# A planned one-core kernel (delta-rule attention and two feed-forward layers): counting instruction blocks in every group

## The chip, the cores and the metric

The program runs on one core of a Trainium2 chip. The metric is the device time of one execution in microseconds (us). Before the change it is 1174.78 us, the median of 3 runs (1173.24 to 1175.62).

## The reference

```python
# attention: B, H, S, D = 4, 8, 768, 48; a state matrix of 48x48 for each of 32 heads, step by step in time
k_n = k / (norm(k) + 1e-06)
for t in range(S):
    y[:, :, t] = einsum('bhd,bhde->bhe', q[:, :, t], state)
    v_old = einsum('bhde,bhd->bhe', state, k_n[:, :, t])
    state = state + beta[:, :, t] * einsum('bhd,bhe->bhde', k_n[:, :, t], v[:, :, t] - v_old)
x = y as 3072 tokens of 384
# first feed-forward layer, 1536 wide
x = (silu(x @ w_gate) * (x @ w_val)) @ moe_w_out
# second, 2048 wide
h = x @ w_in
out = where(h > 0, h, exp(min(h, 0)) - 1) @ moe2_w_out
```

The weights come as 64-bit floats and are taken apart on the chip.

## The kernel before

**Tiling.** The 3072 tokens are worked on in 12 groups g of 256. A group is 128 time steps of two batches, which makes 16 heads (u), cut into four chunks (c) of 32 steps that lie on the four 32-row quarters of the 128 partitions. `a` is the batch within the group, `par` the parity of a head.

**Attention steps of a group**, each one call of `add`: loads of k, q, v; norms of k (`norm`, L453 to L500); transposes of q and k on PE (tr, L538); products of k with k and q (gram, L570), masked by DVE into `gr`; inversion of the 32x32 triangles on DVE (`invert`, L630/L637, in groups 0 to 2 the half-size form L647/L653, joined by products j1 at L678 and j2 at L694); x (L741); g (`gstep`, L761), whose result is copied to `lc` (L770, a helper `put`); the chain of states over the chunks (L795, DVE adds at L801); y (L829); transposes of y (xtr, L853), which give the feed-forward input `xh`, `xl`. These are float32 products on 32-row corners of the array: each stands in the trace as two loads of weights and two products.

**Feed-forward.** `moe1` gives 24 projections (L995, runs of 9 products 128x256) and 12 output products (L1021, runs of 9) for each group. `moe2` (L1107, L1144) runs behind all groups.

**What sets the order.** Nothing is issued as it is written. `add` records a step with the engines that may do it and its readers and writers, and `Order.run` plans all engines' orders with its own times. `wait` orders a step behind the readers of a name as well, `r` only behind its last writer. PE's instruction stream is counted in blocks of 256 (`BLOCK`, counter `at`, a load and a product being two). `fetch(t, occ, n, keep)` says how late a step would come if it passes into a block that has not arrived; before the change it returns 0 for every time after `UNTIL` = 170e3 ns. Where a PE step would come over `STALL` late, `run` takes a short feed-forward step instead, if there is one. `JOIN` names kinds of steps (2: transposes, 4: chain, 5: y) whose two halves (a = 0, 1) are one step in groups after the first. Before 170 us the planner fills idle time of PE with products that nobody reads: `fill` (L1174, 128x512) and `fill2` (L1184), and ahead of a gap of over 6 us `quick` (L1179, 61 products of 16 columns), which runs the stream up to the next block's limit.

Of the kernel before, what the change touches and what calls it, by code (L numbers as in the profile page):

```python
# [45 lines left out]
class Order:  # L46
# [54 lines left out]
    def fetch(self, t, occ, n, keep):  # L101

        at, full, late = self.at, self.full, 0.0
        if t > self.until:
            return 0.0
        if not keep:
            full = dict(full)
        x = t
        end = at + n
        while at // self.BLOCK != end // self.BLOCK:  # L110
            b = at // self.BLOCK + 1
            x += occ * (b * self.BLOCK - at) / n
            at = b * self.BLOCK
            w = max(0.0, full.get(b, 0.0) - x)
            late += w
            x += w
            m = at - self.LEAD
            if m >= self.at:
                y = t + occ * (m - self.at) / n
            else:  # L120
                y = next((a + (m - k) * d for k, a, d in reversed(self.past) if k <= m), x)
            y = max(y, full.get(b, 0.0))
            full[b + 1] = y + self.FETCH[y < self.wire]
        if keep:
            self.past = self.past[-40:] + [(self.at, t, occ / n)]
            self.at = end
        return late

    def run(self, until):
# [22 lines left out]
        while left:  # L152
            best = {}
            for o in ready:
                for e, occ, lat, k, f in o.alts:
                    t = start_of(o, e, occ, lat, k)
# [27 lines left out]
            if e == "PE" and self.fill and t < self.until and left > 1:  # L184
                gap = t - free.get("PE", 0.0)
                if gap > 6000 and k[1] >= 128:
                    n = (self.BLOCK - self.at % self.BLOCK) // 2 + 1
                    self.fetch(t - gap, 28.0 * n, 2 * n, True)
                    self.quick(n)
                    gap -= 28.0 * n  # L190
                n = int(self.share * gap / self.unit)
                if n > 0:
                    late = self.fetch(t - gap, gap, 2 * n, True)
                    t = max(t, t - gap + n * self.unit + late)
                    self.fill(n)
                    kind[0] = k[0]
# [37 lines left out]
def delta_moe_kernel(ctx: ExitStack, tc: tile.TileContext, q, k, v, beta,  # L234
# [11 lines left out]
    C = 4  # L246
# [1 line left out]
    PL1 = 2.5  # L248
    ND = 10
    UNTIL = 170e3  # L250
    JOIN = (2, 4, 5)
    AHEAD = 3
    PAUSE = (0, 'x')
    HOLD = (0, 'm')
# [70 lines left out]
    def act(n, f, psum=True):  # L325
        return [("ACT", (75 if psum else 110) + .8333 * n, (165 if psum else 190) + .8333 * n, 0, f)]
# [4 lines left out]
    def pe(ns, f, kind=0, n=18):  # L331
        return [("PE", ns, ns + 160, (kind, n), f)]
# [115 lines left out]
    def prepare(g, p):  # L448
# [5 lines left out]
        def norm(u0, u1, keys):  # L454
# [12 lines left out]
            add(p, dve(n, lambda: V.tensor_reduce(out=ss[:, u], in_=sq[:, u], op=ALU.add, axis=AX.X)),  # L467
                r=part + ALLA[:3], w=[("ss", x) for x in keys])

            if two:  # L470
                add(p, act(u1 - u0, lambda: A.activation(out=r[:, u], in_=ss[:, u], func=ACTF.Sqrt), False),
                    r=[("ss", x) for x in keys] + ["sqrt"], w=[("sm", x) for x in keys])

# [243 lines left out]
    def attention(g, p):  # L717
# [32 lines left out]
        for a in range(2):  # L750
            for par in range(2):
                h = [Slots(AT if g else AT0, 1) for c in range(C)]

                def gstep(a=a, par=par, h=h):
                    if par == 0:
                        new_lc(a)()
                    for s in range(4):
                        u = a * 8 + 2 * s + par
                        for c in range(C):
                            t = slice(32 * c, 32 * c + 32)  # L760
                            PE.matmul(bank[h[c].got[0]][0:96, s * 80:s * 80 + 80], lhsT=R[t, u, :],  # L761
                                      rhs=gr[t, u, 0:80], start=True, stop=True, skip_group_check=True)
                add(p, pe(860, gstep, 3, 64), r=[(x, n) for x in ("Rk", "Rv") for n in (2 * a, 2 * a + 1)] + [("grk", a), ("grq", a, par)],
                    w=h + ([] if par else lk[a]), need=h,
                    wait=[("lc", a, par, c) for c in range(C)] + (lk[a] if par else []))
                for c in range(C):
                    def put(e, a=a, par=par, c=c, h=h[c]):
                        def f():
# [1 line left out]
                            e(out=buf['lc', a][par][:, :, c, :], in_=pv)  # L770
                        return f

                    add(p, act(320, put(A.copy)) + ([] if g else dve(320, put(V.tensor_copy))), r=[h[c]] + lk[a], w=[("lc", a, par, c)], use=[h[c]])

                def plus(a=a, par=par):
                    b = 64 * par
# [398 lines left out]
                      start=True, stop=True, skip_group_check=True)  # L1175

    def quick(n):
        for _ in range(n):
            PE.matmul(acc[:, 0, 0:16], lhsT=identr, rhs=identr[:, 0:16], start=True, stop=True,  # L1179
                      skip_group_check=True)  # L1180

    def fill2(n):
# [87 lines left out]
```

## Time and profile before

| | |
|---|---|
| median of 3 runs | 1174.78 us (1173.24 to 1175.62) |
| profiled execution, own time | 1170.46 us |
| its span, first to last instruction | 1168.8 us |
| PE busy | 1133.6 us, 97% |
| DVE busy | 779.1 us, 67% |
| ACT busy | 569.3 us, 49% |
| first groups (0 to 170 us), PE busy | 153.84 of 170 us |
| groups with moe1 (170 to 765 us), PE busy | 581.87 of 595 us |
| moe2 (765 to 1168.8 us), PE busy | 397.89 of 403.8 us |

PE is busy nearly all the time, but a busy PE is not at its peak: its small products last some 200 ns each and overlap, so a stretch is read by when the next product starts. Idle time marked "issue" is time in which PE waited for no semaphore that the profile shows. PEclk is the granted clock as a share of 2.4 GHz; it has the levels 0.5 and 1.0.

### The profile page before, as it was taken

To read this page: it belongs to the slowest core of one execution; us is meant where nothing else is said; L and a number is where in the kernel's file an instruction comes from. 1 tells how busy PE (TensorE), PEld (TensorE's weight loads), DVE (VectorE), ACT (ScalarE), POOL (GpSimd) and SP (SyncE) were. 2 spreads that over 40 slices of the span, in tenths; PEclk is the share of its full clock that TensorE was granted. 3 is DMA by queue.
4 is the path that set the end of the run, shared out by engine and by line. 5 is a ranking of instruction groups with operands and counts; after the bars stand their busy time and mean duration, and the time that the engine had idled before them with its cause. 6 is when DMAs were issued, how large, how long until landed. Compare 5 with 4: busy or idle time off the path is not lost.

```text
span 1168.8 us, 34176 instructions
## 1 busy us (share of the span) xinstructions
PE 1133.6 (97%) x14707; PEld 1048.5 (90%) x14707; DVE 779.1 (67%) x2429; ACT 569.3 (49%) x1119; POOL 47.9 (4%) x62
## 2 busy tenths in 40 slices
PE   8889999999999999999999999999999999999998
PEld 7688989998999898989998999989888889888887
DVE  6799858696868686768787743996545344454444
ACT  6599442524242424343434343996545454454443
POOL 2200000000010000000000000000000000000000
PEclk8999999999999999999999999999999999999999
DMA  9480202112020202020200003900101001010000
GB/s 207 127 269 16 43 12 44 33 30 43 16 43 15 44 15 43 9 50 15 44 15 17 15 3 116 371 19 28 55 1 55 1 19 36 1 36 1 27 1 28
DMA packets 106855, 57.34 MB, mean 49 GB/s; under 512 B 76976, under 2 KB 101552, under 8 KB 106704
## 3 DMA queue, kind: packets, MB, share of 16 engines
q1 hardware_dynamic: 106704, 55.16, 17.7%
q8 instruction: 115, 1.88, 0.7%
q14 instruction: 36, 0.29, 0.1%
HBM read 45.71 MB, written 9.44 MB: 47 GB/s over the span
## 4 chain that ended last, share of the span: by engine, by line
PE 86%; DVE 6%; ACT 4%; issue 2%; DMA 1%; SPq 0%; ACTq 0%; DVEq 0%
PE gv L995 24%; PE acc L1021 11%; PE acc L1144 8%; PE at L1144 8%; PE gv L1107 8%; PE at L1107 8%; PE at L761 3%; PE at L795 3%; PE at L741 3%; PE at L570 2%; PE at L829 2%; PE at L538 2%; PE acc L1174 1%; PE acc L1179 1%; DVE ain L661 1%
## 5 line engine op out<-in xcount | busy, mean ns | idle before, releaser
L995 PE MATMUL gv<-xh,w 128*128 128x256 f32 x1728 | 292.6, 288 | 2.0 <-ACT tb L1002 1.4
L995 PEld LDWEIGHTS gv<-xh,w 128*128 128x128 f32 x1728 | 240.0, 191 | 9.0 <-ACT tb L1002 2.0
L1021 PE MATMUL acc<-hb,w 128*128 128x256 f32 x1296 | 184.8, 288 | 0.7 <-issue 0.7
L1021 PEld LDWEIGHTS acc<-hb,w 128*128 128x128 f32 x1296 | 167.8, 194 | 6.2 <-issue 3.7
L995 PE MATMUL gv<-xl,w 128*128 128x256 f32 x864 | 150.6, 283 | 0.3 <-DVE xl L862 0.3
L1002 ACT ACTIVATE tb<-gv 128x256 f32<-128x256 f32 x144 | 55.5, 385 | 189.9 <-PE gv L995 189.9
L995 PEld LDWEIGHTS gv<-xl,w 128*128 128x128 f32 x864 | 124.0, 191 | 0.5 <-DVE xl L862 0.5
L1005 DVE TENSOR_TENSOR tb<-gv,tb 128x256 f32<-128x256 f32 x144 | 60.5, 420 | 78.9 <-ACT tb L1002 51.1
L1009 ACT CAST hb<-tb 128x256 fp32r<-128x256 f32 x144 | 58.7, 407 | 111.5 <-DVE tb L1005 111.5
L1122 DVE SCALAR_TENSOR_TENSOR hb<-gv,hb 128x512 f32<-128x512 f32 x48 | 33.2, 691 | 91.5 <-ACT hb L1119 91.5
L637 DVE TENSOR_TENSOR z<-z,ain 128x60 f32<-128x60 f32 (+32 forms) x522 | 88.5, 209 | 1.1
L630 DVE TENSOR_TENSOR ain<-z,ain 128x60 f32<-128x60 f32 (+32 forms) x522 | 87.7, 205 | 1.0
L1122 DVE SCALAR_TENSOR_TENSOR hb<-at,hb 128x512 f32<-128x512 f32 x48 | 33.1, 690 | 81.0 <-ACT hb L1119 80.9
L1012 DVE TENSOR_TENSOR hb<-tb,hb 128x256 fp32r<-128x256 f32 x144 | 63.9, 444 | 18.4 <-ACT hb L1009 17.7
L1113 ACT ACTIVATE hb<-gv 128x512 f32<-128x512 f32 x48 | 28.7, 597 | 96.5 <-PE gv L1107 96.4
L1119 ACT ACTIVATE hb<-hb,neg 128x512 f32<-128x512 f32 x96 | 69.5, 724 | 2.7
L1113 ACT ACTIVATE hb<-at 128x512 f32<-128x512 f32 x48 | 28.7, 597 | 79.4 <-PE at L1107 79.1
L1116 ACT ACTIVATE hb<-hb 128x512 f32<-128x512 f32 x96 | 60.8, 633 | 2.8
L761 PE MATMUL at<-gr,R 32*96 32x80 f32 x1488 | 45.8, 251 | 0.0
L761 PEld LDWEIGHTS at<-gr,R 32*96 32x96 f32 x1488 | 38.1, 159 | 7.0 <-ACT w L770 0.4
L1144 PE MATMUL acc<-w,ain 128*128 128x384 f32 x192 | 39.6, 340 | 1.8 <-DVE ain L1127 1.3
L1107 PE MATMUL gv<-lc,w 128*128 128x512 f32 x144 | 41.0, 394 | 0.0
(205 smaller groups left out, 2110.6 us busy)
## 6 DMA issues: line engine op xcount, KB each, us to landing
w<-in_moe_w_out_dram SPq DMA_DIRECT2D x28, 384.0 KB, 6.8
w<-in_moe_w_in_dram SPq DMA_DIRECT2D x16, 384.0 KB, 5.8
R<-in_v_dram SPq DMA_DIRECT2D x24, 192.0 KB, 2.8
w<-in_moe_w_gate_dram SPq DMA_DIRECT2D x12, 384.0 KB, 7.5
w<-in_moe_w_val_dram SPq DMA_DIRECT2D x12, 384.0 KB, 7.9
qp<-in_q_dram SPq DMA_DIRECT2D x11, 384.0 KB, 4.7
kp<-in_k_dram SPq DMA_DIRECT2D x11, 384.0 KB, 4.8
x2d<-hb SPq DMA_DIRECT2D x12, 256.0 KB, 2.0
```

The source lines that it names most:

```text
L630: V.tensor_tensor(out=t, in0=z[:, l:l + 1, x:y].to_broadcast([128, l, y - x]), in1=an[:, l, 0:l].unsqueeze(2).to_broadcast([128, l, y - x] ...
L637: V.tensor_tensor(out=z[:, 0:l, x:y], in0=z[:, 0:l, x:y], in1=t, op=ALU.add)
L761: PE.matmul(bank[h[c].got[0]][0:96, s * 80:s * 80 + 80], lhsT=R[t, u, :], rhs=gr[t, u, 0:80], start=True, stop=True, skip_group_check=True)
L995: PE.matmul(dst, lhsT=wt[:, a_, kk * 128:(kk + 1) * 128], rhs=xx[:, kk, :], start=(n == 0), stop=(n == 3 * KD - 1))
L1005: V.tensor_tensor(out=c['s'], in0=bank[h.got[0]][:, TB:2 * TB], in1=c['s'], op=ALU.mult)
L1012: return lambda: e.tensor_tensor(out=c['h'][:, 1, :], in0=c['s'], in1=c['h'][:, 0, :].bitcast(F32), op=ALU.subtract)
L1021: PE.matmul(o_, lhsT=w[:, a_, d * 128:(d + 1) * 128], rhs=c['h'][:, b_, :], start=(f == 0 and n == 0 and d != 1), stop=(f == F1 - 1 and n ...
L1107: PE.matmul(x, lhsT=W[f][:, 0, a_, kk * 128:(kk + 1) * 128], rhs=x2[n][b_][:, kk, :], start=(m == 0), stop=(m == 3 * KD - 1))
L1116: A.activation(out=c['r'], in_=c['r'], func=ACTF.Exp, scale=-1.0)
L1119: A.activation(out=c['r'], in_=c['r'], func=ACTF.Identity, bias=neg1, scale=1.0)
L1122: V.scalar_tensor_tensor(out=c['r'], in0=bank[h.got[0]], scalar=0.0, in1=c['r'], op0=ALU.max, op1=ALU.add)
L1144: PE.matmul(o, lhsT=c['h'][:, b_, t * 128:(t + 1) * 128], rhs=W[f][:, 1][:, a_, :], start=(f == 0 and m == 0), stop=(f == F2 - 1 and m == 2))
```

## The change

It has five parts. `fetch` counts blocks at all times, and when it only asks (keep False) it adds how late the following block would come, were the rest of the block run at 59 ns an instruction. `quick` issues float32 products of 32x32 corners with 16 columns in place of 128x128 ones, half as many calls, and its count is rounded. `JOIN` keeps the chain alone, so that transposes and y are planned in halves. `norm` of group 1 takes a square root on ACT as group 0 does, where it had Newton steps on DVE. `gstep` with par = 1 waits for the last writer of `lc` and not for its readers, and the copies of g's result may go to DVE as well as to ACT in every group.

```diff
@@ fetch
-        if t > self.until:
-            return 0.0
...
             y = max(y, full.get(b, 0.0))
             full[b + 1] = y + self.FETCH[y < self.wire]
+        if not keep:
+            b = at // self.BLOCK + 1 if at == end else end // self.BLOCK + 1
+            rest = (b * self.BLOCK - end) * 59.0
+            return late + max(0.0, full.get(b, 0.0) - (t + occ + late) - rest)
@@ run
-                    n = (self.BLOCK - self.at % self.BLOCK) // 2 + 1
+                    n = (self.BLOCK - self.at % self.BLOCK) // 4 * 2 + 2
                     self.fetch(t - gap, 28.0 * n, 2 * n, True)
                     self.quick(n)
@@
-    JOIN = (2, 4, 5)
+    JOIN = (4,)
@@ norm
-            if two:
+            if g < 2:
                 add(p, act(u1 - u0, lambda: A.activation(out=r[:, u], in_=ss[:, u], func=ACTF.Sqrt), False),
@@ gstep
-                add(p, pe(860, gstep, 3, 64), r=[(x, n) for x in ("Rk", "Rv") for n in (2 * a, 2 * a + 1)] + [("grk", a), ("grq", a, par)],
+                add(p, pe(860, gstep, 3, 64), r=[(x, n) for x in ("Rk", "Rv") for n in (2 * a, 2 * a + 1)] + [("grk", a), ("grq", a, par)] + (lk[a] if par else []),
                     w=h + ([] if par else lk[a]), need=h,
-                    wait=[("lc", a, par, c) for c in range(C)] + (lk[a] if par else []))
+                    wait=[("lc", a, par, c) for c in range(C)])
...
-                    add(p, act(320, put(A.copy)) + ([] if g else dve(320, put(V.tensor_copy))), r=[h[c]] + lk[a], w=[("lc", a, par, c)], use=[h[c]])
+                    add(p, act(320, put(A.copy)) + dve(320, put(V.tensor_copy)), r=[h[c]] + lk[a], w=[("lc", a, par, c)], use=[h[c]])
@@ quick
-        for _ in range(n):
-            PE.matmul(acc[:, 0, 0:16], lhsT=identr, rhs=identr[:, 0:16], start=True, stop=True,
+        for x in range(n // 2):
+            r = slice(32 * (x % 4), 32 * (x % 4) + 32)
+            PE.matmul(acc[r, 0, 0:16], lhsT=ident[r, r], rhs=ident[r, 0:16], start=True, stop=True,
```

In the changed file every line from 104 to 121 stands two lower, and from 122 on two higher in number (L761 is L763), at the end three (L1174 is L1176, L1179 is L1182).

Three places of the order. First, PE at the start of the program, between the last gram of group 0 and the first x: L1179 and L1182 are `quick`, L1174 and L1176 `fill`, L678 and L680 j1. Before:

```order
L570 MATMUL at_88<-kq 32x64 x16
L570 MATMUL at_85<-kq 32x64 x16
L1179 MATMUL acc<-identr 128x16 x61
L1174 MATMUL acc<-identr 128x512 x34
L678 MATMUL at_86<-ain,gr 32x32 x32
```

After:

```order
L572 MATMUL at_88<-kq 32x64 x16
L572 MATMUL at_85<-kq 32x64 x16
L1182 MATMUL acc<-ident 32x16 x31
L1176 MATMUL acc<-identr 128x512 x33
L680 MATMUL at_86<-ain,gr 32x32 x32
```

The row of 61 products with 128 rows has become a row of 31 with 32 rows (two passes each), and the fill is one shorter.

Second, PE in a middle group, where the trace of before stands at 459 to 466 us: chain (L795, L797; its dt and l are the two buffers of a = 1), gram (L570, L572), a run of 9 output products (L1021, L1023) or of 18 projections (L997), and y (L829, L831). Before:

```order
L795 MATMUL at_88<-sv,dt_1617 48x48
L795 MATMUL at_88<-sv,l_68_1618 48x48
L570 MATMUL at_85<-kq 32x64 x16
L1021 MATMUL acc<-hb_268_7414,w_36_1021 128x256 x9
L829 MATMUL at_86<-st,lc_626 32x48
L829 MATMUL at_86<-sv,lc_626 32x48 x3
```

After:

```order
L797 MATMUL at_87<-sv,dt_1647 48x48
L797 MATMUL at_87<-sv,l_73_1648 48x48
L997 MATMUL gv_82<-xh_245_6761,w_54_1349 128x256 x3
L997 MATMUL gv_82<-xl_246_6762,w_54_1349 128x256 x3
L997 MATMUL gv_82<-xh_245_6761,w_54_1349 128x256 x6
L997 MATMUL gv_82<-xl_246_6762,w_54_1349 128x256 x3
L997 MATMUL gv_82<-xh_245_6761,w_54_1349 128x256 x3
L831 MATMUL at_86<-st,lc_595 32x48
L831 MATMUL at_86<-sv,lc_595 32x48 x3
```

Before, gram stands between the last chain step and 9 products, and y is one run of 128 passes; after, 9 products stand ahead of that chain step, 18 behind it, and 9 more between the two halves of y.

Third, DVE at the norms of group 1, about 44 us in the trace of before: L467 (L469) sums the squares, L483 to L490 are the first Newton steps, L477 (L479) is the reciprocal. Before:

```order
L467 TENSOR_REDUCE sm_77<-ain 128x16
L770 COPY w_18_657<-gv_83 96x4x80
L483 TENSOR_SCALAR sm_78<-sm_77 128x16
L778 TENSOR_TENSOR w_18_657<-w_18_657,kq 48x16x32
L770 COPY lc_626<-at_87 96x4x80
L770 COPY lc_626<-at_85 96x4x80
L488 SCALAR_TENSOR_TENSOR sm_79<-sm_78,sm_77 128x16
L489 TENSOR_TENSOR sm_79<-sm_79,sm_78 128x16
```

After:

```order
L469 TENSOR_REDUCE sm_77<-ain 128x16
L772 COPY lc_595<-gv_83 96x4x80
L809 COPY sv<-at_86 48x4x48
L780 TENSOR_TENSOR lc_595<-lc_595,kq 48x16x32
L477 TENSOR_SCALAR sm_79<-sm_79 128x16
L479 RECIPROCAL sm_78<-sm_79 128x16
```

The Newton steps are gone; the reciprocal follows the sum with three other operations between.

Over the whole program the order holds 14707 loads and as many products on PE before and 14710 after; runs of attention products between feed-forward or fill products are 126 before and 121 after; copies on ACT fall from 382 to 317 and copies on DVE rise from 36 to 101; loads of ACT's tables are 3 in both.

## Rows read from the trace of the kernel before

**Rows 1.** The page: span, and busy time of each engine.

```profile
span 1168.8 us, 34176 instructions
PE 1133.6 (97%) x14707; PEld 1048.5 (90%) x14707; DVE 779.1 (67%) x2429; ACT 569.3 (49%) x1119; POOL 47.9 (4%) x62
```

**Rows 2.** PE's waits, 170 to 765 us: us in total, times, longest.

```profile
PE at L570 <- issue: 5.5, 4, 2.5
PE at L829 <- issue: 3.1, 5, 1.0
PE at L795 <- issue: 1.6, 1, 1.6
PE at L741 <- DVE ain L661: 1.0, 5, 0.3
```

**Rows 3.** Stretches A:B: length, PE, PEld, DVE, ACT, POOL busy (count), PEclk, DMA, GB/s.

```profile
51.13:57.32 6.19, 3.34 (x137) 2.41 (x132) 5.76 (x16) 4.76 (x8) 2.35 (x2) 1.00 1.09 339
86.96:90.30 3.34, 2.57 (x129) 2.35 (x128) 3.03 (x4) 2.88 (x5) 1.05 (x1) 0.77 0.02 5
184.00:187.50 3.50, 3.50 (x69) 3.27 (x71) 3.40 (x14) 0.39 (x1) 0.27 (x1) 0.51 0.00 0
291.61:295.61 4.00, 2.98 (x128) 2.66 (x128) 3.42 (x9) 0.87 (x2) 0.53 (x1) 1.00 0.03 7
350.00:375.00 25.00, 24.06 (x326) 23.64 (x327) 22.55 (x126) 6.54 (x17) 0.32 (x1) 1.00 0.01 2
```

**Rows 4.** Timeline: start, us, engine, line, operation, form, count, idle before and releaser.

```profile
12.70 9.47 PE L1179 MATMUL acc<-identr 128*128 128x16 f32 x61
...
22.02 10.36 PE L1174 MATMUL acc<-identr 128*128 128x512 f32 x34
...
24.02 0.77 DVE L671 STREAM_TRANSPOSE ain<-ain 128x256 f32<-128x256 f32 x2
...
32.30 1.31 PE L678 MATMUL at<-ain,gr 16*32 16x32 f32 x128
33.10 0.48 DVE L685 SCALAR_TENSOR_TENSOR z<-at,zd,eye 128x256 f32<-128x256 f32 x1 [7.47 <-PE at L678]
...
33.64 0.75 PE L694 MATMUL at<-ain,z 32*32 32x32 f32 x64
...
42.40 0.49 DVE L770 COPY lc<-gv 96x320 f32<-96x320 f32 x1 [1.50 <-PE at L761]
...
57.32 0.20 PE L829 MATMUL at<-sv,w 96*32 96x48 f32 x1 [2.44 <-issue]
...
182.70 0.44 PE L570 MATMUL at<-kq 48*32 48x64 f32 x17 [1.42 <-issue]
...
637.65 0.57 PE L570 MATMUL at<-kq 48*32 48x64 f32 x22 [0.62 <-issue]
```

**Rows 5.** The chain that ended last: start, us, what and how many.

```profile
106.47 1.08 PE gv L995 x9
...
184.57 1.92 PE acc L1021 x9
...
211.93 2.78 PE at L741 x128
...
243.56 2.16 PE gv L995 x18
...
274.63 2.34 PE gv L995 x18
...
399.94 0.85 PE at L795 x32
...
465.72 2.27 PE at L829 x128
...
638.22 2.22 PE acc L1021 x9
```

**Rows 6.** Gram by line: out<-in, form, count, busy us, mean ns, idle before.

```profile
L570 PE MATMUL at<-kq 48*32 48x64 f32 x1536 | 24.9, 219 | 6.1 <-issue 5.5 <-ACT kq L541 0.5
```

## The prediction

> **What bounds the kernel now.** I read the page first: PE is busy 1133.6 of 1168.8 us, DVE 67% and ACT 49% [rows 1]. So a gain must come out of PE's own row: the few places where it stands idle, those where it does nothing useful, and those where it runs at half its clock.
>
> PE's waits in the groups with moe1 come next [rows 2]. Hardly any of them is for data: 1.0 us for DVE's inversion ahead of x. But 10.2 us, in ten waits, are "issue", in the middle of attention steps whose operands are there. The stretches between two such waits that follow each other tell what they are [rows 3]: from 86.96 to 90.30 us and from 291.61 to 295.61 us PE passes 128 loads and 128 products each, that is 256 instructions. Counted in the program's order, all issue waits of over 0.25 us but none of the waits for data stand a whole number of 256 instructions apart. So a block of 256 instructions can't be passed in less than 3.3 to 4.0 us; a block that has less work of its own ends in a wait. The Trainium skill speaks against that reading: "Runtime: NRT & Kernel Launch", section "Instruction fetch mechanics", has the stream refilled in blocks of 256 as well, but calls the cost of crossing a limit mostly hidden and the fetch hidden by the rate of issue. By that rule the waits would have another cause and the change would take none of them away; the traces of before disagree, with 2.5 us for the longest [rows 2]. It is weighed as a rival below.
>
> Third, the start [rows 4]. DVE ends the last turn for j1 at 24.02 + 0.77 = 24.79 us. PE begins j1 at 32.30 us, since 61 quick products (9.47 us) and 34 fill products (10.36 us) stand ahead of it in its row, and nobody reads them. DVE then waits 7.47 us for j1. This is 7.5 us in which neither engine is kept by data.
>
> **The change part by part.**
>
> *Quick, at the start.* 31 float32 corner products are 62 passes. The nearest row is j2 with 64 passes of the same 32x32 corners in 0.75 us [rows 4]: 62 take 0.7 us in place of 9.47. The 33 fill products take 33/34 of 10.36 = 10.1 us. PE would be through at 12.70 + 0.7 + 10.1 = 23.5 us, and j1 could begin at 24.9, as soon as DVE's turn is seen: 7.4 us earlier. But the quick products end at a block's limit, and the next block may not be there. In 51.13 to 57.32 us, with the DMAs as full as here (339 GB/s), one block took 6.2 us [rows 3]. The block before this limit is entered some 1.3 us ahead of 12.70, so the next would come at 17.6, the fill would end at 27.7, and j1 gain 4.6 us. With a block in 4.0 us, the slowest in rows 3 with idle DMAs, it is 15.4 and 25.5: 6.8 us. I take j1 at 27.1, gain **5.2 us**; the DMAs are busy here, so nearer to the first. Bounds: 7.4 us with no wait for the block; and 0.2 us, if it comes only at 22.0, where PE passed the limit before. What is late next: DVE's `mid` (L685) follows j1 directly, and x, the copies, and the loads of weights behind x move with it. From there to 125 us PE, DVE and ACT are all nearly full, and all three are freed earlier by the same time, so I let it pass through.
>
> *Block limits in group 0.* The wait of 2.44 us at 57.32 stands inside y [rows 4]. Y is now in two halves, with a chain step, transposes and fill between them, so the block that ends there holds more. The steps wait for each other here anyway. I take **-1.2 us**, between 0 and -2.4.
>
> *Block limits in groups 1 and 2.* There j1, j2 and x still follow each other closely. Their blocks hold as little as before or less, but j1, j2 and x also wait for DVE and ACT between. **+0.5 us**, from -0.5 to +1.5.
>
> *Block limits from 170 to 765 us.* I add up what each block of 256 holds, by the rows' prices: x 2.78/128, y 2.27/128, chain and g 0.85/32, gram 24.9/1536 us a pass, a feed-forward product 2.16/18 = 0.12 us [rows 5, 6], a 128-row transpose as one of those, and 0.18 us more where feed-forward follows attention (2.34 against 2.16 for 18 products, rows 5). In the order of before, 17 blocks hold less than 3.7 us (the middle of 3.3 and 4.0) and lack 11.0 us together; 10.2 us of waits were measured. In the order of the change 7 blocks are left that lack 2.6 us, the worst 0.95 us where two chain steps, gram and y meet in group 2. That leaves 10.2 x 2.6/11.0 = 2.4 us: **-7.8 us**, bounds -5 and -10.
>
> *The clock.* From 184.0 to 187.5 us the granted clock is 0.51, the 1.2 GHz level, right behind a wait of 1.42 us at a limit [rows 3, 4]; through gram, its row before was busy with small products alone. Nine products take 1.92 us there, against 1.08 at the full clock; y, with 128 passes in 2.27 us, is no slower [rows 5]. Four such falls follow limits, the first at 182.7 and the last at 637.7 us [rows 4]; the five runs of nine that they hit (184.57 to 638.22 in rows 5) lose 3.9 us over 5 x 1.08. Most of these limits lose their wait and gain feed-forward work around them. **-2.9 us**, one fall left; bounds 0 and -3.9.
>
> *PE's own work.* Runs of attention fall from 126 to 121, each worth 0.18 us: -0.9. Four more products of fill2 cost 0.5. **-0.4 us** (-1 to +1).
>
> *Copies and closer steps.* 65 copies go from ACT to DVE, 0.49 us each there [rows 4]: 32 us more for DVE in 11 groups, 2.9 us each. DVE has that time on the average, less so during an inversion, where it is busy 22.55 of 25 us [rows 3]. And where y and its transposes were apart by a feed-forward run, the transposes now often follow the second half of y at once, which must cover the first half's copy, 0.49 us by the nearest row. In the order, x stands as far behind gram as before in most groups (some 30 us of PE's work). What hides these is the same feed-forward work as before. I take **+1.5 us**, bounds 0 and +5.9 (12 groups by 0.49). In group 1 ten small Newton operations leave DVE and one square root comes to ACT, with no further table load: within these bounds.
>
> The moe2 part is the same work in the same order: nothing.
>
> Sum: -5.2 - 1.2 + 0.5 - 7.8 - 2.9 - 0.4 + 1.5 = **-15.5 us**. The profiled execution took 1170.46 us, so 1155.0 for one like it; the median of the runs is 1174.78, 4.3 us above, and the forecast is set against that: **1159 us**.
>
> **The rivals.**
>
> *The limits are not the cause* (the rule of instruction fetch above, as a mechanism of this kernel: PE halts inside attention steps for something that moves with them). For: the profile names no releaser. Against: the spacing of 256. Then the terms -1.2, -7.8 and -2.9 fall away and +0.5 too: 1174.8 - 5.2 - 0.4 + 1.5 = 1170.7.
>
> *The start gives nothing*, because corner products cost about what the full ones did (155 ns), or because the block behind them comes only at 22 us. For: the rows have no float32 corner product with 16 columns. Against: 64 passes in 0.75 us. 1159 + 5.2 = 1164.5.
>
> *DVE becomes the bound, and the kernel slower.* The 2.9 us of copies in each group delay the masks and the inversion, and x waits on PE. For: 22.55 of 25 us busy, and x already waits for the inversion five times [rows 2]. Against: those waits are 1.0 us together. If all of it comes through, 11 x 2.9 = 32 us are added to 1174.8 - 17: 1190. It turns the sign from 17/11, about 1.5 us in each group.
>
> *Everything comes at the good end.* No late block at the start, hardly a limit left, no falls of the clock, group 0 shorter: -24 us, 1151.
>
> **How the numbers follow.** Forecast with its terms between their middles (1153 to 1166) 0.60; limits not the cause 0.08; start gives nothing 0.12; DVE the bound 0.06; the good end 0.14. The range of 1148 to 1169 us takes in the good end, the missing start, and the forecast with +5 for the copies and -5 for the limits; it leaves out the slower case and most of the first rival. A measurement here tells about 0.2%, 2.4 us, from no change. Faster by more: the forecast, the start rival, the good end and part of the first rival, 0.89; within: 0.05; slower: 0.06.
>
> **What would show it.** In the changed kernel j1 of group 0 should begin near 27 us and DVE's wait ahead of L687 fall from 7.47 us to 2 or 3; quick should be one short row. Issue waits of PE from 160 to 760 us should sum to 2 to 4 us, and the granted clock fall there at most twice. PE's waits for DVE and ACT should stay under 4 us in that part; DVE's busy share should rise by some 30 us. The forecast is wrong if j1 starts at 30 us or later, if issue waits stay in number and only move, or if x waits for L663 by over 1 us in each group.

## The result, and the profile after

The changed kernel takes 1162.03 us, the median of 4 runs (1159.94 to 1163.22); the kernel before took 1174.66 us beside it (4 runs, 1173.24 to 1175.62). The ratio is 0.9892 [0.9872, 0.9911], 12.6 us less, where 1159 us were forecast. The profiled execution, the fastest of the four, took 1159.94 us with a span of 1158.2 us, 10.5 us less than that of before. All positions below are from the profiled executions. Two slow runs, one of before (2903.75 us) and one of a_trim (1339.70 us), count in the medians below but in no ratio.

The page of the kernel after, to be held against [rows 1] (busy us, share of the span, instructions):

```profile
span 1158.2 us, 34199 instructions
PE 1122.1 (97%) x14710; PEld 1034.8 (89%) x14710; DVE 802.2 (69%) x2482; ACT 554.2 (48%) x1056; POOL 52.2 (5%) x62
```

PE has the same work and is busy 11.5 us less; DVE is busy 23.1 us more, the copies that it took over less the Newton steps that left it.

| | before | after | difference so far |
|---|---|---|---|
| j1 of group 0 | 32.3 | 28.1 | -4.2 |
| x of group 1 | 87.9 | 83.8 | -4.1 |
| x of group 2 | 154.8 | 150.2 | -4.6 |
| first product of moe2 | 757.8 | 746.5 | -11.3 |
| end of the span | 1168.8 | 1158.2 | -10.6 |

So the gain has two places: the first 28 us, and the groups with moe1 between 155 and 745 us. Between 28 and 150 us next to nothing is won, and moe2 gives 0.7 us back.

The start, in the timeline of the kernel after (start, us, engine, line, operation, form, count, idle before and releaser), against [rows 4]:

```profile
12.49 0.69 PE L1182 MATMUL acc<-ident 32*32 32x16 f32 x61
...
17.79 0.23 PE L1182 MATMUL acc<-ident 32*32 32x16 f32 x1 [4.60 <-issue]
17.95 10.19 PE L1176 MATMUL acc<-identr 128*128 128x512 f32 x33
...
23.82 0.77 DVE L673 STREAM_TRANSPOSE ain<-ain 128x256 f32<-128x256 f32 x2
...
28.07 1.31 PE L680 MATMUL at<-ain,gr 16*32 16x32 f32 x128
28.87 0.48 DVE L687 SCALAR_TENSOR_TENSOR z<-at,zd,eye 128x256 f32<-128x256 f32 x1 [3.44 <-PE at L680]
```

61 of the 62 quick passes take 0.69 us in place of 9.47. Then PE stands 4.60 us at the limit, the 33 fill products end at 28.1, and DVE, whose turn was done at 24.59, waits 3.44 us in place of 7.47.

PE's waits of the kernel after, 160 to 755 us (us in total, times, longest):

```profile
PE at L797 <- issue: 3.8, 3, 1.6
PE at L743 <- DVE ain L663: 1.5, 6, 0.3
PE at L540 <- ACT dt L772: 1.3, 4, 0.6
PE gv L997 <- ACT tb L1004: 1.1, 2, 0.9
PE at L831 <- issue: 0.9, 1, 0.9
PE at L572 <- DVE sv L803: 0.7, 4, 0.2
PE at L540 <- DVE dt L772: 0.4, 2, 0.2
```

The same view of before has the four lines of [rows 2] and three more:

```profile
PE gv L995 <- ACT tb L1002: 0.9, 1, 0.9
PE at L853 <- issue: 0.4, 1, 0.4
PE at L538 <- ACT lc L770: 0.3, 1, 0.3
```

The issue waits fell from 10.6 us in eleven to 4.7 us in four, and none stands in gram (L572) any more. The waits for data rose from 2.2 to 5.0 us.

The windows view of the kernel after (stretch, length, busy us and count of PE, PEld, DVE, ACT, POOL, then PEclk, DMA share and GB/s): the middle of the program, and the last 128 products ahead of each of the four limits that wait.

```profile
155.00:745.00 590.00, 580.25 (x9744) 552.55 (x9733) 461.47 (x1833) 227.26 (x536) 31.14 (x35) 1.00 0.19 47
...
233.95:237.14 3.19, 2.42 (x146) 2.06 (x133) 3.11 (x8) 1.41 (x3) 0.53 (x1) 1.00 0.02 5
286.39:289.93 3.54, 2.65 (x131) 2.38 (x129) 0.85 (x2) 1.27 (x3) 0.00 (x0) 1.00 0.03 5
342.37:347.88 5.51, 3.87 (x138) 3.46 (x132) 5.27 (x15) 0.00 (x0) 0.52 (x1) 1.00 0.79 89
451.88:457.02 5.14, 3.78 (x135) 3.38 (x129) 4.92 (x14) 0.00 (x0) 0.52 (x1) 1.00 0.81 93
```

PEclk is 1.00 over the whole middle part: the falls to the 1.2 GHz level in which before ran five of its runs of nine [rows 5] are gone. And of the four blocks, two were passed in 3.2 and 3.5 us with idle DMAs; the other two, with DMAs at 89 and 93 GB/s, took 5.5 and 5.1. What these carry there is the next group's k and q, as the DMA queue of SP shows for the first of them (start, us, line, what is loaded from where):

```profile
339.57 0.37 SPq L434 DMA_DIRECT2D kp<-in_k_dram  x1
341.06 0.37 SPq L440 DMA_DIRECT2D qp<-in_q_dram  x1
```

The blocks themselves are in the trace. The page of the kernel after lists a DMA queue of instructions (packets, MB, share of the 16 engines): 115 packets of 16 KB, as many as PE's 29420 loads and products make blocks of 256.

```profile
q8 instruction: 115, 1.88, 0.7%
```

Asked in narrow windows, the DMA view places each packet. From 342.4 to 345 us it shows data alone (a packet counts where it starts, so a share can pass 100%), and from 345 to 348 us the block for which PE waits at 347.88:

```profile
q1 hardware_dynamic: 2281, 0.43, 150.0%
...
q8 instruction: 1, 0.02, 3.0%
```

At all four limits such a packet has landed 1.4 to 1.5 us before PE goes on. It starts 0.6 to 0.7 us after PE has entered the block in front where the DMAs are idle, and 2.7 and 2.1 us after it where k and q are loaded. So these waits are for a block of instructions, and there it is mainly the start of its transfer that comes late.

Last, two pieces of the chain that ended last, in the kernel after (start, us, what and how many):

```profile
392.29 1.26 PE acc L1023 x9
...
399.70 1.08 PE acc L1023 x9
```

Nine products take 1.26 us at the full clock where they follow attention (g, as here), and 1.08 where they follow other feed-forward.

### The profile page after: what moved, and what is told of

Read it like the earlier page. It is cut to its first block, busy times and chain, and to the rows that moved or that the text cites. A ratio compares the mean times of both kernels' runs of the same rounds, so it can differ in the third digit from the quotient of the medians.

```text
span 1158.2 us, 34199 instructions
## 1 busy us (share of the span) xinstructions
PE 1122.1 (97%) x14710; PEld 1034.8 (89%) x14710; DVE 802.2 (69%) x2482; ACT 554.2 (48%) x1056; POOL 52.2 (5%) x62
## 4 chain that ended last, share of the span: by engine, by line
PE 60%; DVE 4%; ACT 2%; issue 1%; ACTq 0%; DVEq 0%
PE gv L997 14%; PE acc L1146 8%; PE gv L1109 8%; PE at L1146 8%; PE at L1109 8%; PE acc L1023 7%; PE at L797 1%; PE at L743 1%; PE at L763 1%; PE at L831 1%; PE at L572 1%; PE at L540 1%; PE at L855 0%; ACT hb L1121 0%; DVE hb L1124 0%
## 5 line engine op out<-in xcount | busy, mean ns | idle before, releaser
L997 PE MATMUL gv<-xh,w 128*128 128x256 f32 x1728 | 290.8, 287 | 2.9 <-ACT tb L1004 2.0
L997 PEld LDWEIGHTS gv<-xh,w 128*128 128x128 f32 x1728 | 239.4, 191 | 9.5 <-ACT tb L1004 3.1
L1023 PE MATMUL acc<-hb,w 128*128 128x256 f32 x1296 | 183.3, 287 | 0.0
L1023 PEld LDWEIGHTS acc<-hb,w 128*128 128x128 f32 x1296 | 166.5, 193 | 2.8 <-ACT hb L1011 0.2
L997 PE MATMUL gv<-xl,w 128*128 128x256 f32 x864 | 150.4, 283 | 0.2 <-DVE xl L864 0.2
L997 PEld LDWEIGHTS gv<-xl,w 128*128 128x128 f32 x864 | 123.8, 191 | 0.4 <-DVE xl L864 0.4
L763 PE MATMUL at<-gr,R 32*96 32x80 f32 x1480 | 45.4, 251 | 0.2 <-DVE w L772 0.2
L763 PEld LDWEIGHTS at<-gr,R 32*96 32x96 f32 x1480 | 37.8, 159 | 7.0 <-DVE w L772 0.4
```

What stands on the lines that cost most here:

```text
L997: PE.matmul(dst, lhsT=wt[:, a_, kk * 128:(kk + 1) * 128], rhs=xx[:, kk, :], start=(n == 0), stop=(n == 3 * KD - 1))
L1023: PE.matmul(o_, lhsT=w[:, a_, d * 128:(d + 1) * 128], rhs=c['h'][:, b_, :], start=(f == 0 and n == 0 and d != 1), stop=(f == F1 - 1 and n ...
```

## The experiments

Each table row gives the median, the ratio to the kernel before on the same chip with its 95% interval, and from the profiled execution the start of j1 in group 0, of x in group 2 and of moe2, PE's issue waits in 160 to 755 us, and the falls of the granted clock to the 1.2 GHz level between 155 and 1100 us (start, length). The experiments ran in three sets on three chips, so a kernel is set against after by these ratios: 0.001 of them is 1.17 us.

| kernel | median us | ratio | j1 | x, group 2 | moe2 | issue waits | falls |
|---|---|---|---|---|---|---|---|
| before | 1174.66 | 1 | 32.3 | 154.8 | 757.8 | 10.6 | four of 3.4 |
| after | 1162.03 | 0.9892 [0.9872, 0.9911] | 28.1 | 150.2 | 746.5 | 4.7 | none |
| b_quick | 1168.32 | 0.9955 [0.9941, 0.9970] | 28.2 | 150.8 | 754.4 | 9.5 | 286 (6.8), three of 3.4 |
| a_oldquick | 1167.21 | 0.9947 [0.9931, 0.9964] | 34.7 | 158.0 | 755.4 | 4.2 | 158 (6.8) |
| a_trim | 1159.43 | 0.9876 [0.9852, 0.9899] | 25.9 | 148.6 | 746.5 | 4.8 | 346 (3.4) |
| a_ahead | 1166.31 (1 run) | - | 26.8 | 155.4 | 752.9 | 3.9 | three of 3.4 |
| a_shift | 1165.23 | 0.9938 [0.9915, 0.9961] | 28.5 | 153.2 | 752.8 | 2.7 | 348 (3.4), 457 (6.8) |
| a_nocount | 1172.70 | 0.9988 [0.9969, 1.0007] | 27.6 | 150.8 | 754.8 | 7.1 | 227 (10.2), 558 (6.8) |
| b_count | 1178.87 | 1.0048 [1.0029, 1.0066] | 34.9 | 162.8 | 767.5 | 7.1 | 370 (6.8), 613 (10.2), three of 3.4 |
| a_join | 1170.72 | 0.9966 [0.9946, 0.9986] | 27.7 | 156.1 | 761.2 | 1.6 | 306 (6.8), 555 (6.8), two of 3.4 |
| a_norm | 1164.34 | 0.9933 [0.9906, 0.9960] | 28.3 | 153.7 | 753.2 | 5.8 | 460 (3.4), 624 (3.4) |
| a_wait | 1162.74 | 0.9915 [0.9889, 0.9940] | 28.8 | 154.6 | 751.2 | 5.9 | 399 (3.4) |
| a_act | 1158.07 | 0.9860 [0.9834, 0.9886] | 29.0 | 150.6 | 745.7 | 0.9 | none |
| a_both | 1153.18 | 0.9835 [0.9810, 0.9860] | 24.5 | 146.2 | 740.6 | 0.9 | none |

### The start: is the gain that of the quick products, and what is late next?

**b_quick** is the kernel before with the new quick row alone, **a_oldquick** the kernel after with the old one.

```diff
-                    n = (self.BLOCK - self.at % self.BLOCK) // 2 + 1
+                    n = (self.BLOCK - self.at % self.BLOCK) // 4 * 2 + 2
...
-        for _ in range(n):
-            PE.matmul(acc[:, 0, 0:16], lhsT=identr, rhs=identr[:, 0:16], start=True, stop=True,
+        for x in range(n // 2):
+            r = slice(32 * (x % 4), 32 * (x % 4) + 32)
+            PE.matmul(acc[r, 0, 0:16], lhsT=ident[r, r], rhs=ident[r, 0:16], start=True, stop=True,
```

> The kernel before, with the corner products of quick alone; order and block limits otherwise as before. Theory (start): quick takes 0.7 us, the block behind it is late as in the changed kernel (4.6 us), j1 begins near 28.1 us in place of 32.3 and all that follows moves with it: 1174.7 - 4.2 = 1170.5 us. Rival (the start is given back before 125 us, since loads and decoding of weights set the pace): 1173 to 1175 us. Issue waits from 170 us on stay at about 10 us in both.

> The changed kernel with the quick products of before (128 rows). Theory (start): j1 back at 32.3 us, 1162.0 + 4.2 = 1166.2 us; issue waits after 160 us stay near 4.7 us. Rival (the start is given back): 1162 to 1163 us.

Alone it gives 5.1 us (1168.32 against 1173.43), and taken back it costs 1167.21 against 0.9892 x 1173.43 = 1160.8, so 6.4 us. In b_quick j1 begins at 28.2 and x of group 1 at 83.9, as in after: the 4.1 us of j1 pass through 55 us of full engines undiminished. Its issue waits in the groups with moe1 stay near before's (9.5 us against 10.6 in that stretch). The start and the middle are two separate gains. That the time gains 5 to 6 us where j1 gains 4.2 has to do with the old row, which is not of one length: its 61 products took 9.47 us in the profile of before, at a granted clock of 0.72, and 12.04 us in that of a_oldquick, at 0.55, where j1 came only at 34.7.

Behind the quick row stands the wait for the block. **a_ahead** lets fewer loads of weights run ahead (AHEAD is how many of them don't wait for x of group 0); it ran once, so its time isn't compared.

```diff
-    AHEAD = 3
+    AHEAD = 1
```

> The changed kernel with one load of weights ahead of x of group 0 in place of three (AHEAD = 1), for one look at the start: the DMAs carry less between 9 and 17 us. Theory (the block behind quick is late because the DMAs are full): PE's wait at the end of quick falls from 4.6 us to 2.5 or less, j1 comes 2 us earlier than 28.1. Rival (a block takes that long after a run of corner products whatever the DMAs do): the wait stays at 4 to 5 us. The time as a whole may be longer, since weights come later.

Its timeline at the start, and below it the windows view of 9 to 17.5 us (columns as above):

```profile
13.55 0.69 PE L1182 MATMUL acc<-ident 32*32 32x16 f32 x61
16.63 0.23 PE L1182 MATMUL acc<-ident 32*32 32x16 f32 x1 [2.39 <-issue]
...
26.81 1.31 PE L680 MATMUL at<-ain,gr 16*32 16x32 f32 x128
```

```profile
9.00:17.50 8.50, 6.11 (x207) 5.32 (x206) 5.78 (x21) 7.21 (x8) 1.63 (x3) 0.85 1.04 187
```

The same window of the kernel after:

```profile
9.00:17.50 8.50, 3.44 (x197) 3.08 (x197) 6.29 (x23) 7.22 (x8) 1.11 (x2) 0.93 1.14 317
```

With 187 GB/s in place of 317 the wait is 2.39 us in place of 4.60; gram and the quick row ahead of it take as long as in after. One run is thin, but the instruction queue shows the same: the packet starts 1.4 us after PE has entered the block in front, and 3.7 to 3.9 us after it in after and in the other kernels with the new row and 317 GB/s. So the block comes late because the DMAs carry weights at that time, for about half of the wait. j1 gains 1.3 us by it and not 2.2, since gram ends 1.1 us later here; the kernel as a whole shows no gain.

**a_trim** shortens the fill that follows: 18 of the 33 products with 512 columns become 18 passes of corner products.

```diff
+                m = 18 if gap < t - free.get("PE", 0.0) else 0
...
-                    self.fill(n)
+                    self.fill(n - m)
+                    self.quick(m)
```

> The changed kernel, order and instruction count kept, with 18 of the 33 fill products behind quick replaced by 18 passes of corner products. Theory (start): the row of PE ends near 23 us, j1 begins when DVE's turn is done, 24.7 in place of 28.1 us: 1162.0 - 3.4 = 1158.6 us. Rival (DMA and the decoding of weights set the pace behind the start): 1161 to 1162 us. Rival (without the long fill the clock is low when j1, j2 and x come, and they take twice as long): 1162 us or more.

j1 begins at 25.9 us, although in this profile the block took longer still (a wait of 5.18 us); the ratio is 0.9876 against 0.9892, a gain of some 2 us that the intervals alone don't separate. What was late next at the start was thus the block, and behind it the fill, as the prediction's 17.6 and 27.7 us had it.

### The middle: are the limits the cause?

**a_shift** puts 64 passes that nobody reads, and that the planner doesn't count, into one output product of group 0. Order and work behind them stay, but each limit falls 128 instructions earlier in the row.

```diff
             def prod(f=f, c=c, g=g):
...
+                if g == 0 and f == 1:
+                    for x in range(32):
+                        r = slice(32 * (x % 4), 32 * (x % 4) + 32)
+                        PE.matmul(acc[r, 1, 256:272], lhsT=ident[r, r], rhs=ident[r, 0:16], start=False,
+                                  stop=True, skip_group_check=True)
```

> The changed kernel, its order kept, with 64 passes of corner products (128 instructions, about 0.5 us) put once ahead of the second run of output products of group 0, which the planner does not count: every later limit of 256 stands 128 instructions earlier in the same order. Theory (limits): the waits move to other steps, 128 instructions away from where they were modulo 256; by the prices of the prediction 12 blocks now lack 7.8 us in place of 7 that lack 2.6, so the issue waits after 160 us go from 4.7 to some 9 us and the time to 1162.0 + 0.5 + 4.5 = 1167 us, more if the clock falls behind them. Rival (the waits belong to the steps in which they stand): same steps, same 4.7 us, 1162.5 us.

Two of the four waits in the timeline of the kernel after:

```profile
347.88 0.20 PE L797 MATMUL at<-sv,l 96*48 96x48 f32 x1 [1.64 <-issue]
...
457.02 0.20 PE L797 MATMUL at<-sv,l 96*48 96x48 f32 x1 [1.36 <-issue]
```

The same places in a_shift:

```profile
347.15 0.64 PE L572 MATMUL at<-kq 48*32 48x64 f32 x29 [0.29 <-issue]
...
457.27 1.08 PE L572 MATMUL at<-kq 48*32 48x64 f32 x32 [0.47 <-issue]
458.28 2.29 PE L1028 MATMUL acc<-hb,w 128*128 128x256 f32 x9
```

The chain steps run through, and PE halts inside gram some 64 products earlier: the waits go where the count goes, and nothing in the steps themselves makes PE halt. That was the rival "the limits are not the cause", and it falls. The size I got wrong: with the planner's limits in the wrong places I expected far more issue waits than in after, and there were 2.7 us against 4.7. So this run does not show that the planner spares waits by knowing where the limits are. The time still rose by 0.0046, 5.4 us. Two places show it: x of group 1 begins at 87.4 in place of 83.8 (the limits of groups 0 and 1 moved too, and one now stops j1 for 2.7 us), and the clock fell behind both waits above. The window behind the second one, in a_shift:

```profile
457.20:464.00 6.80, 6.73 (x82) 6.24 (x82) 5.50 (x15) 0.00 (x0) 0.53 (x1) 0.50 0.18 22
```

PE worked for 6.8 us at the 1.2 GHz level; the nine output products in it take 2.29 us, and nine in after take 1.26.

**a_nocount** takes the counting behind 170 us, and the look at the following block everywhere, out of after; **b_count** puts these two into before and changes nothing else (its diff is the reverse).

```diff
+        if t > self.until:
+            return 0.0
...
-        if not keep:
-            b = at // self.BLOCK + 1 if at == end else end // self.BLOCK + 1
-            rest = (b * self.BLOCK - end) * 59.0
-            return late + max(0.0, full.get(b, 0.0) - (t + occ + late) - rest)
```

> The changed kernel with the planner's counting of blocks cut off at 170 us again and without the look at the following block; all other parts of the change stay. Theory (counting takes the limit waits away): 13 blocks lack 12.3 us by the prices of the prediction, issue waits after 160 us come back to about 10 us (4.7 in the changed kernel), the clock falls two to four times, and the time is 1162.0 + 5.5 + 2.5 = 1170 us. Rival (the halves of y and of the transposes and the wait taken off g did it, not the counting): issue waits near 5 us, 1162 to 1164 us.

> The kernel before with the counting of blocks in every group and the look at the following block, no other part. Theory (the planner needs the halves to place feed-forward runs between): with y and the transposes still in one piece 10 blocks lack 9.7 us, against 17 that lack 11.0 before; issue waits after 160 us fall from 11 to about 9 us, 1174 - 2 = 1172 us. Rival (counting alone does it): issue waits near 5 us, 1166 to 1167 us.

Without the count, after loses nearly all its gain: 0.9988, with limit waits in three kinds of steps, gram, chain and y (waits of PE, a_nocount, 160 to 755 us):

```profile
PE at L570 <- issue: 3.0, 2, 1.5
PE at L795 <- issue: 2.5, 3, 1.0
PE at L829 <- issue: 1.6, 2, 0.9
```

From x of group 2 to moe2 it needs 7.7 us more than after. Of these 2.4 are issue waits; its waits for data are 5.0 us as in after. The rest goes with two falls of the clock, 17.1 us together, and with its order, and was not told apart.

But the count alone makes the kernel before slower, 1.0048, which I had not expected. Its issue waits did fall, from 10.6 to 7.1 us in that stretch, and others came (waits of PE, b_count, same stretch):

```profile
PE at L831 <- issue: 4.4, 4, 1.9
PE at L572 <- issue: 2.7, 2, 1.4
PE gv L997 <- DVE xl L864: 2.6, 3, 1.8
PE gv L997 <- ACT xh L861: 1.3, 3, 0.6
```

PE now waits for xh and xl, the feed-forward's own input, and the clock fell five times between 155 and 1100 us. Still, the stretch as a whole is only 1.7 us longer than in before, 604.7 us from x of group 2 to moe2. The larger loss lies ahead of it, where the look at the following block acts as well: from j1 to x of group 2 b_count needs 127.9 us against 122.5, at a granted clock of 0.93 against 0.97. Its late j1 is the old row again, 11.81 us at 0.57.

**a_join** is after with transposes and y joined again.

```diff
-    JOIN = (4,)
+    JOIN = (2, 4, 5)
```

> The changed kernel with y and the transposes planned in one piece for both halves again (JOIN of kinds 2, 4, 5). By the order, 7 blocks lack 3.9 us (2.6 in the changed kernel) and 133 runs of attention stand in place of 121. Theory: issue waits after 160 us 5 to 6 us, runs +12 x 0.18 = 2.2 us, data waits 1 to 2 us less than 5.0 since y's copy and the transposes have more room: 1163 to 1164 us. Rival (the halves are what spares the limits): issue waits over 8 us, 1167 us or more.

Again PE waits for xh and xl (waits of PE, a_join, same stretch):

```profile
PE gv L997 <- DVE xl L864: 4.4, 3, 1.6
...
PE gv L997 <- ACT xh L861: 1.5, 3, 0.6
```

The issue waits are only 1.6 us, less than in after, yet 8.7 us of the gain are gone (0.9966). Both my theories missed that. Here too a part is lost early: from j1 to x of group 2 a_join needs 128.4 us, after 122.2. The way I read the waits, and this was argued and not tried: with joined halves the planner has to put its feed-forward runs ahead of the limits in larger lots, uses up the projections of one group, and stands at the next one's xh and xl before the transposes have given them. Whatever the reason, the count needs the halves. From x of group 2 to moe2 before takes 603.0 us, the count without the halves 604.7 (b_count) and 605.1 (a_join), the halves without the count 604.0 (a_nocount), and both together 596.3 (after).

### The smaller parts

**a_norm** gives group 1 its Newton steps back, **a_wait** makes g with par = 1 wait again for the readers of `lc` (`lk[a]` goes back from r to wait), **a_act** leaves the copies of g's result to ACT alone behind group 0.

```diff
-            if g < 2:
+            if two:
```

> The changed kernel with the Newton steps of group 1 back on DVE. By the order 10 blocks lack 6.3 us in place of 7 that lack 2.6, 117 runs of attention. Theory A (the root on ACT frees DVE in the stretch where groups 0 and 1 wait for it): x of group 1 comes 1 to 2 us later, issue waits after 160 us about 6 to 7 us: 1165 us. Rival B (the norms' part has no price of its own, only the plan's luck with limits counts): x of group 1 within 0.5 us, 1162 to 1164 us.

```diff
-                    wait=[("lc", a, par, c) for c in range(C)])
+                    wait=[("lc", a, par, c) for c in range(C)] + (lk[a] if par else []))
```

> The changed kernel with g of par = 1 planned behind the readers of lc again. By the order 8 blocks lack 3.4 us, 121 runs, 8 products of fill2 fewer. Theory (the false wait only kept g's steps apart, and feed-forward stands between them anyway): 1161 to 1164 us, data waits as in the changed kernel, 5 us. Rival (the wait taken off is worth something): g's four steps of a group take over 1 us longer each time, 1168 us or more.

```diff
-                    add(p, act(320, put(A.copy)) + dve(320, put(V.tensor_copy)), r=[h[c]] + lk[a], w=[("lc", a, par, c)], use=[h[c]])
+                    add(p, act(320, put(A.copy)) + ([] if g else dve(320, put(V.tensor_copy))), r=[h[c]] + lk[a], w=[("lc", a, par, c)], use=[h[c]])
```

> The changed kernel with the copies of g's result on ACT alone from group 1 on, as before the change. By the order, 154 runs of attention in place of 121, 6 blocks that lack 4.6 us. Theory (the copies on DVE let the planner keep runs long, their cost is hidden): 33 x 0.18 = 6 us more of PE's own work, 1168 us. Rival (DVE's copies delay masks and inversion): data waits fall from 5.0 to 3 us or less and the time stays at 1161 to 1163 us.

The Newton steps cost 0.9933 - 0.9892, 4.8 us, though the two intervals just overlap. j1 of group 1, which waits for DVE's turn, comes at 78.9 in place of 76.2, and x of that group at 86.1 in place of 83.8; so 2.3 us come with DVE, and the rest with another order behind it (falls at 460 and 624 us). The square root on ACT is thus likely a part of its own, where the prediction put it within the bounds of the copies. The false wait has no price that can be told: 0.9915, with an interval that holds 0.9892.

The copies on DVE were the surprise. With ACT alone the kernel is at least not slower, 0.9860 [0.9834, 0.9886] against after's 0.9892; its order has 154 runs of attention products in place of 121, and yet PE's busy time rises by only 1.9 us (waits of PE, a_act, 160 to 755 us, all that the view lists):

```profile
PE gv L997 <- ACT tb L1004: 1.5, 2, 1.3
PE at L572 <- DVE sv L803: 1.0, 4, 0.3
PE at L743 <- DVE ain L663: 1.0, 3, 0.4
PE at L855 <- ACT y L838: 1.0, 2, 0.7
PE at L797 <- issue: 0.9, 1, 0.9
```

Here one limit is left, and the waits for data are no more than in after. As I read it, it isn't the engine of the copies that counts: with another engine for them the planner finds another order, and this one spreads the feed-forward runs more finely. The engine and the order were not tried apart.

**a_both** puts a_act's and a_trim's edits together.

> The changed kernel with two edits that were each faster by themselves: copies of g's result on ACT alone from group 1 on, and 18 of the 33 fill products at the start replaced by corner passes. Theory (the two are in different places, and the start is handed on): ratio 0.986 less some 2.5 us, about 0.984 of before, 1155 us where before is 1173.8. Rival (the decoding of weights behind the start takes the gain of the shorter fill, since ACT now has the copies): 1158 us.

It takes 1153.18 us (1152.73 to 1154.55, 5 runs), 0.9835 [0.9810, 0.9860], close to the 0.984 of its theory, and it beats both kernels: its whole interval lies below the lower end of after's. The timeline of its start, quick and fill at L1184 and L1178, j1 at L682:

```profile
18.14 6.20 PE L1178 MATMUL acc<-identr 128*128 128x512 f32 x15
24.28 0.36 PE L1184 MATMUL acc<-ident 32*32 32x16 f32 x18
24.52 1.31 PE L682 MATMUL at<-ain,gr 16*32 16x32 f32 x128
```

## Why the prediction was right, step by step

The sign and the two places of the gain came as forecast, the time 3 us above 1159. The terms, from the profiled executions and the experiments:

**Quick at the start**, forecast -5.2, measured -4.2 at j1 and 5 to 6 us in the time (b_quick, a_oldquick). The choice that mattered was the one between the block in 4.0 us and the block with full DMAs: it came at 17.79, where the row with 339 GB/s said 17.6. I had taken a value between the two; the row whose DMA share was like that of the place was the one to take whole. That j1 passes through to x is confirmed.

**Limits in groups 0 to 2**, forecast -0.7 together, measured -4.6 + 4.2 = -0.4 at x of group 2. Inside it the steps were larger: the first projection came 6.8 us earlier, 2.6 more than j1, since the wait of 2.44 us inside y [rows 4] is gone. But x of group 1 was again only 4.1 us ahead. From 30 to 165 us the issue waits fell from 7.3 to 4.5 us, and the waits for data rose from 4.7 to 6.9. One of these is j1's wait for DVE's inversion in group 1 (waits of PE in the kernel after, 70 to 80 us):

```profile
PE at L680 <- DVE ain L673: 1.5, 1, 1.5
```

In before this wait is 1.7 us.

**Limits in the groups with moe1**, forecast -7.8, measured -5.9 (10.6 to 4.7; the forecast began at 10.2): this is the term that was mis-sized. The failing step is "17 blocks hold less than 3.7 us": one price for every block. The blocks that end at 347.88 and 457.02 us hold 55 chain passes, 9 feed-forward products and 64 passes of gram, by the prediction's prices 1.46 + 1.26 + 1.04 = 3.8 us, so they were counted as lacking nothing. They took 5.51 and 5.14 us, at a DMA share of 0.8, while the next group's k and q were loaded; the two with idle DMAs took 3.2 and 3.5. In before the limit at 57.3 us was one of this kind [rows 3], so the price had been there to be read. It isn't a clean rule: in a_shift two blocks that end in the same loads (193 GB/s) were passed in 3.2 and 3.4 us. There the packets of instructions started 0.5 and 0.8 us after the blocks in front were entered, in after 2.7 and 2.1; why the same loads hold back the one and not the other is open. The sum of what blocks lack orders the kernels only roughly: 11.0 for before (10.2 measured), 12.3 for a_nocount (7.1), 7.8 for a_shift (2.7), 2.6 for after (4.7).

That the limits were the cause at all went against the Trainium skill, "Runtime: NRT & Kernel Launch", section "Instruction fetch mechanics", which calls the cost of a limit mostly hidden. The trace decides against it here: the waits move with the count in a_shift, they are up to 1.64 us each in after, and each ends 1.4 to 1.5 us behind the landing of a block.

**The clock**, forecast -2.9 with one fall left; in after's profile there was none. The price was a little too high as well: nine products behind attention take 1.26 us at the full clock, not 1.08, so the five runs had lost 9.3 - 6.3 = 3.0 us and not 3.9. The gain is about -3.0. In a_shift, b_count, a_nocount and a_join falls are there again, so this term is a part of what an order gives, and not a remainder. A part of it is the luck of a run: a_trim, which differs from after in the fill of the first 28 us alone, has one fall.

**Own work, copies and closer steps**, forecast +1.1 together. The waits for data rose from 2.2 to 5.0 us, +2.8: the inversion ahead of x 0.5, the copies of g's result ahead of the transposes (L540) 1.4, the states ahead of gram (L572) 0.7 and the tables of the activation (L997 behind ACT's tb) 0.2. That is over the 1.5 taken for them and within the bound of 5.9. The price of 0.18 us for a run of attention is too high for the whole program: a_act has 33 runs more, needs 595.1 us from x of group 2 to moe2 against after's 596.3, with 3.8 us less of limit waits; that leaves 2.6 us, about 0.08 for a run if nothing else differs. The order's own runs, 126 to 121, and the products of fill2 were not measured apart.

**From x of group 2 to moe2** the forecast had -7.8 - 2.9 + 1.1 = -9.6; measured are -5.9 - 3.0 + 2.8 = -6.1 by terms, -6.7 by the two positions. **moe2**, forecast at nothing, took 0.7 us more: 411.7 us against 411.0, and the other kernels with the same moe2 take 410.9 to 412.0.

Of the marks, j1 came at 28.1 (27 forecast), DVE's wait at 3.44 (2 to 3), issue waits at 4.7 (2 to 4), the falls at none (at most two), the waits for data at 5.0 (under 4), and DVE's busy time at +23 (+30). The rivals: "the start gives nothing" falls by b_quick, "the limits are not the cause" by a_shift, "DVE becomes the bound" by after itself, where x waits 1.5 us in six places for the inversion, and "everything comes at the good end" by the 4.60 us of the first block and the four limits left.

The profiled executions differ by 10.5 us and the medians by 12.6: that of before lies 4.2 us under its median, that of after 2.1. The forecast's 15.5 us were worked out from the profile of before and then taken off the median, so by the terms they are 5 us too many, and 2.1 us of that were made good by luck. The clock shows where these come from. Its mean is 0.985 in the profiled execution of before, while the medians of its runs on the three chips of the experiments are 0.980 to 0.983; in after it is 0.992 and 0.991. At some 0.7 us for 0.001 of the clock (see the last section) that is an estimated 1 to 3 us.

## What to carry to other kernels

Where an engine's waits have no releaser, count its instructions between them: if the spacing is that of the fetch blocks, shifting the whole row by half a block shows in one run whether the limits are the cause, and the queue of instructions in the DMA view shows when each block came. Price a block by the load of the DMAs at its place, not by one figure. And where a planner makes the order, test its parts in pairs: here the count alone lost 0.5%, all the rest without it gained nothing that can be told from 0, and both together gave 1.1%. And give the position of each stage for every run, or a loss at the start is read as one in the middle.

## What was not expected of the hardware

**Instruction blocks share the DMAs with the data.** With idle DMAs PE passed 128 products up to a waiting limit in 3.2 to 3.5 us, with the loads of the next group in 5.1 and 5.5; at the start the wait is 4.60 us at 317 GB/s and 2.39 at 187. The blocks are packets of 16 KB in a DMA queue of their own (q8), and what varies most is how late such a packet starts.

**Some short halts are followed by a fall of the clock, others are not.** In a_shift waits of 0.29 and 0.47 us inside gram were followed by 3.4 and 6.8 us at the 1.2 GHz level; in after's profile waits of 1.64 and 1.36 us inside the chain were not. The first of these two places has a wait of 1.92 us in a_trim, and there 3.4 us at the 1.2 GHz level follow. What sets this is open.

**The spread of the runs goes with the order.** The kernel before spreads over 11 us on one chip (1168.26 to 1179.40 in 29 runs), a_nocount and a_join over 7 and 9 (12 runs each); a_act spreads over 2.7 us (1156.00 to 1158.73, 6 runs) and a_both over 1.8 (5 runs). The mean granted clock, which is on record for every run, goes with it: 0.975 to 0.988 in the 29 runs of before, 0.982 to 0.994 in those of a_join, but 0.992 to 0.994 in a_act and 0.992 to 0.995 in a_both. Within the runs of before the time falls by some 0.7 us for 0.001 of the clock (correlation -0.88), within those of a_join by 0.75 (-0.96). So the kernels that spread are those whose clock falls more in some runs than in others. Why a run has more falls is open.
